# Attention beside a long convolution on one core: the opening in smaller pieces, with new numbers for the planner

## The chip, the core and the metric

The kernel runs on one core of a Trainium2 chip. The core has engines that each work through a list of instructions in order and meet at semaphores: TensorE (PE, matrix products into the eight PSUM banks), ScalarE (ACT, functions of single elements), VectorE (DVE, arithmetic on tiles), GpSimd (POOL, here for setting memory and starting transfers) and SyncE (SP, here for starting transfers). The metric is the time of one execution on the device in microseconds (us), as the median of several runs. The profile is of one further execution.

## The reference

Two independent blocks, each on 2,048 tokens with 512 features, whose results stand side by side in the output. The first is attention with 32 heads of 16 features; the second multiplies shifted keys by values and convolves the product along the tokens with one filter of length 2,048 for each feature.

```
qkv = (x @ wqkv) -> q, k, v        # 32 heads of 16 features
scores = q @ k^T * 16 ** -0.5      # 32 x 2048 x 2048
a = (softmax(scores) @ v) -> (2048, 512) @ wo

k_shift = sum over 4 taps of shifted k * shift_k
kv = k_shift * v
y = causal convolution of kv with ssm_k  (by FFT in the reference)
b = q * (y + kv * ssm_D)
out = concatenate(a, b)
```

The costly part is the exponential of the 32 x 2048 x 2048 scores.

## The kernel before, in words

**Tiling.** The scores are cut into 2,048 blocks of 128 keys by 512 queries of one head. Heads are processed in groups of four that sit 32 partitions apart, of which a key matmul uses one strip of 32; a pass `n` is one group of four heads with one block of 512 queries, and there are 32 passes. For each block PE computes scores (L775), an engine takes the exponential, and PE multiplies it with the values (L912), summing in bank `PVB` over the 16 key tiles. A column of ones beside the values gives the softmax's denominator in the same matmul; at the end of a pass DVE transposes the sums (L981), divides and transposes back.

**Two engines for the exponential.** ACT reads two or three banks at once (L800, tile `PT`), three banks for even steps and three for odd ones. DVE computes other blocks by an approximation in four operations (L861, L868 twice, L873, tile `PTD`); such a block's scores come either in bank `BGB`, beside the three of ACT, or in the place of ACT's third bank, so that ACT has two in that step.

**Work between.** Projections of later heads (L485, L494, L517), the shifted keys (L506), the convolution (L1127, as matmuls with filter rows that SP loads into `WR`) and the output projection (L1055) are placed on PE between score groups. Where room is left, filler matmuls of zeros (L1322) keep PE busy.

**What sets the order.** All instruction lists are written out when the kernel is built. A planner keeps a clock for each engine and goes through steps `T`: it emits a step's scores and its exponential (`emit_qk`), value products of the step two before (`pv_step`), perhaps one more block for DVE (`late_block`), background work (`emit_bg`), transfers (`release`) and filler (`warm_up`). Constants at the top of the file are its limits. `LATE_D` says how long PE may be held by a late block, `LATE` how long a DVE block must be done before its value product is placed, `OVER_C`, `HURRY`, `HALF`, `TURN` and `NEAR` by how much a piece of background work may run over, `OPEN` and `CLOSE` how early it is taken up, `GAP` and `T_DVE` where DVE blocks are allowed, `S_U` how much of other DVE work goes ahead of an urgent operation, `N_TAIL` how many last steps have two blocks alone, and `MOST_OP` how many pieces of the output projection a step of the end may take. In such a step of two blocks the third bank belongs to the output projection.

**The opening.** DVE sets `JNK` (for an early load of ACT's table) and a zero tile in `PT`; PE multiplies the zero tile eight times (`warm`, L624) and then spreads a pattern for the mask `MASK` (L632). ACT's queue loads the first 128 columns of the q and k weights, SP's queue transposes x's first 512 tokens into `xT` in two transfers of 256, then loads the v weights and the rest of x. `first` (L639) makes q of tokens 0 to 255 in bank 6, k of the same in bank 7, and q of tokens 256 to 511 in bank 5. DVE multiplies q by the mask for even and odd heads (L649), ACT copies the keys (L653). The first step's scores need keys and queries of tokens 0 to 255; the second step's also need queries 256 to 511 for even heads. Keys from 256 on come as a unit of background work (L494, copied at L542).

The transfers of x are issued by these lines:

```
    load_x(0, 2)
    h_wv = [dma(sp, d_w[2], WV[:, :, 0:128], wview[:, :, 2 * D:2 * D + 128], kb=128, late=1.8)]
    load_x(1)
    load_x(2)
    load_x(3)
```

## Time and profile before

| | us |
|---|---|
| median of 3 runs (lowest, highest) | 818.57 (818.21, 819.93) |
| the profiled execution | 822.45 |
| its span, first to last instruction | 820.71 |
| first exponential on ACT begins | 9.23 |
| last stretch of exponentials ends | 815.79 |
| exponentials on ACT, three blocks / two blocks | 456 / 202 |
| blocks on DVE | 276 |
| filler matmuls on PE | 602 |

The page shows busy time by engine, the chain of work that ended last, and the costliest groups of instructions. "Idle before" is the time in which an engine stood still ahead of an instruction, with the work that ended the wait. ACT is the fullest engine, so the time is read best as its list: when it begins, what its instructions take, where it stands still, and what follows the last one. PE waits for ACT before 447 groups of scores, 186.0 us in all: there the delay is PE's, and it costs nothing.

### The profile page before, as it was taken

How to read it: one execution, taken by the hardware profiler on the slowest of the kernel's cores; microseconds unless marked ns; L12 is line 12 of the kernel's file. 1: busy time of each engine (PE TensorE's matmuls, PEld its weight loads, DVE VectorE, ACT ScalarE, POOL GpSimd, SP SyncE). 2: the span in 40 equal slices, each digit the busy share in tenths (PEclk: the TensorE clock that was granted, in tenths of full speed). 3: DMA queues.
4: the chain of work that ended last, by engine and by line, in shares of the span. 5: the costliest groups of instructions: out<-in, count | busy, mean ns of one | idle time of the engine just before them, and what ended most of it. 6: DMA issues, size and time to landing. Idle time of an engine off the chain costs nothing.

```text
span 820.7 us, 31039 instructions
## 1 busy us (share of the span) xinstructions
PE 737.6 (90%) x14084; PEld 328.8 (40%) x14084; DVE 786.7 (96%) x1383; ACT 801.7 (98%) x662; POOL 87.6 (11%) x160
## 2 busy tenths in 40 slices
PE   8889999999987988989898999999989989999887
PEld 3333434444342443434443444344433333434244
DVE  4999999999997999999999999999999979999996
ACT  6999999999998999999999999999999999999997
POOL 6200211010100101000011010101001102010000
PEclk9999999999999999999999999999999999999999
DMA  9896077768577684265678286677787582663100
GB/s 233 187 299 194 8 162 253 263 194 270 190 267 257 236 280 150 53 205 186 237 236 266 72 266 239 229 258 244 259 254 240 181 279 93 214 221 109 53 2 28
DMA packets 88882, 161.39 MB, mean 197 GB/s; under 512 B 50256, under 2 KB 53968, under 8 KB 88368
## 3 DMA queue, kind: packets, MB, share of 16 engines
q1 hardware_dynamic: 81760, 150.43, 57.2%
q0 software_dynamic: 5792, 8.66, 3.5%
q8 instruction: 111, 1.82, 0.9%
q10 hardware_dynamic: 1200, 0.33, 0.2%
q14 instruction: 19, 0.16, 0.1%
HBM read 142.61 MB, written 6.42 MB: 182 GB/s over the span
## 4 chain that ended last, share of the span: by engine, by line
ACT 86%; DVE 6%; PE 5%; issue 1%; DMA 1%
ACT PT L800 86%; DVE EH L868 2%; PE PS L775 2%; DVE PTD L873 1%; DVE FX L861 1%; PE PS L912 1%; PE PS L1127 1%; DMA xT<-in_A_x_dram 1%; PE PS L494 0%; PE PS L639 0%; DVE OUTA L1063 0%; PE PS L517 0%; DVE DT L981 0%; PE PS L1055 0%; DVE YB L1147 0%
## 5 line engine op out<-in xcount | busy, mean ns | idle before, releaser
L800 ACT ACTIVATE PT<-PS 128x1536 bf16<-128x1536 f32 (+1 forms) x658 | 799.4, 1527 | 8.2 <-PE PS L775 7.9
L775 PE MATMUL PS<-QT,KTo 32*128 32x512 bf16 (+2 forms) x2248 | 261.4, 366 | 55.7 <-ACT PT L800 23.9
L912 PE MATMUL PS<-PT,VA 128*32 128x512 bf16 (+2 forms) x1948 | 195.6, 370 | 11.4 <-issue 6.1
L873 DVE SCALAR_TENSOR_TENSOR PTD<-EH,FX 128x512 uint16<-128x512 f32 x276 | 185.3, 677 | 5.2 <-PE PS L912 5.0
L861 DVE TENSOR_SCALAR FX<-PS 128x512 f32<-128x512 f32 x276 | 187.5, 681 | 2.0 <-PE PS L775 1.7
L868 DVE SCALAR_TENSOR_TENSOR EH<-EH 128x512 f32<-128x512 f32 x276 | 183.8, 677 | 0.0
L868 DVE SCALAR_TENSOR_TENSOR EH<-FX 128x512 f32<-128x512 uint16 x276 | 181.9, 682 | 0.1
L1127 PE MATMUL PS<-WR,KV 128*24 128x128 bf16 (+8 forms) x8192 | 171.5, 220 | 0.2 <-issue 0.2
L775 PEld LDWEIGHTS PS<-QT,KTo 32*128 32x128 bf16 x2248 | 68.5, 91 | 228.8 <-ACT PT L800 186.0
L1127 PEld LDWEIGHTS PS<-WR,KV 128*32 128x32 bf16 (+7 forms) x8192 | 135.5, 95 | 43.9 <-issue 21.7
L1322 PE MATMUL PS<-IDN,ZW 128*32 128x512 bf16 (+3 forms) x602 | 131.1, 313 | 1.5 <-DVE DT L981 1.2
L347 POOL DMA_DIRECT2D QT<-QS x120 | 58.4, 494 | 461.0 <-DVE QS L533 411.1
L912 PEld LDWEIGHTS PS<-PT,VA 128*32 128x32 bf16 x1948 | 49.3, 93 | 113.3 <-issue 94.8
L912 PE MATMUL PS<-PTD,VA 128*32 128x512 bf16 (+1 forms) x300 | 87.0, 369 | 1.7 <-DVE PTD L873 1.7
L1322 PEld LDWEIGHTS PS<-IDN,ZW 128*32 128x32 bf16 x602 | 49.2, 96 | 45.5 <-issue 14.9
L347 POOL DMA_DIRECT2D out_dram<-OUTA x15 | 8.2, 549 | 150.5 <-DVE OUTA L1063 144.2
L912 PEld LDWEIGHTS PS<-PTD,VA 128*32 128x32 bf16 x300 | 22.5, 95 | 3.5 <-DVE PTD L873 2.6
L981 DVE STREAM_TRANSPOSE DT<-PS 128x512 f32<-128x512 f32 x31 | 21.9, 707 | 1.5 <-PE PS L912 1.3
L517 PE MATMUL PS<-WKV,xT 128*128 128x128 bf16 x256 | 17.6, 220 | 2.2 <-DVE FX L861 0.9
L1147 DVE CAST YB<-PS 128x256 bf16<-128x256 f32 x32 | 13.4, 417 | 6.0 <-PE PS L1127 5.0
L494 PE MATMUL PS<-xT,WKV 128*128 128x512 bf16 (+1 forms) x64 | 17.6, 385 | 1.4 <-DVE KV L555 0.7
L1055 PE MATMUL PS<-WKV,OTN 128*128 128x512 bf16 (+1 forms) x68 | 18.0, 370 | 0.4 <-DVE OTN L1030 0.3
(69 smaller groups left out, 226.6 us busy)
## 6 DMA issues: line engine op xcount, KB each, us to landing
WR<-kz_scratch SPq DMA_DIRECT2D x256, 512.0 KB, 5.7
KV<-KV SPq DMA_DIRECT2D x16, 256.0 KB, 5.7
kz_scratch<-WR SPq DMA_DIRECT2D x1, 2176.0 KB, 8.3
QN<-in_B_q_dram POOLq DMA_DIRECT2D x2, 1024.0 KB, 8.6
out_dram<-QN POOLq DMA_DIRECT2D x2, 1024.0 KB, 8.5
QT<-QS POOLq DMA_DIRECT2D x120, 16.0 KB, 1.9
out_dram<-OUTA POOLq DMA_DIRECT2D x15, 128.0 KB, 2.2
QN<-in_B_ssm_k_dram SPq DMA_DIRECT2D x1, 1024.0 KB, 9.1
```

The costliest lines, as they stand in the source:

```text
L347: f(outp, inp).then_inc(dsem.sem, 16)
L494: return e.matmul(PS[:, bank, c0:512], lhsT=WK[:, dc, o * 128:(o + 1) * 128], rhs=xT[:, dc, sc * 512 + c0:(sc + 1) * 512], start=(dc == 0) ...
L775: ins = e.matmul(PS[:, bank, i * w:i * w + w], lhsT=KTo[32 * s:32 * s + 32, OF[n_] % 2, kt * 128:(kt + 1) * 128], rhs=QT[32 * s:32 * s + 3 ...
L800: h_exp[T] = act.op(lambda e: e.activation(PT[:, p0:p0 + n, :].rearrange("p b f -> p (b f)"), PS[:, banks[0]:banks[0] + n, :].rearrange("p ...
L861: h_f = urgent(lambda e: e.tensor_scalar(fx, PS[:, bank, :], FIX_ADD, FIX_HI, ALU.add, ALU.min), [h, h_last.get(i - R_FX)], slack=S_FX)
L868: st["h"] = dve.op(lambda e: e.scalar_tensor_tensor(eh, src, (P1, P2)[j], src, ALU.add, ALU.mult), [st["h"], h_last.get(i - R_EH)], us=us)
L873: lambda e: e.scalar_tensor_tensor(out16, eh, P3, fx, ALU.mult, ALU.add),
L912: ins = e.matmul(dst, lhsT=w, rhs=rhs, start=first, stop=last, tile_position=(0, 32 * s))
L981: h_t = urgent(lambda e: e.transpose(out=dt, in_=PS[:, PVB, :]), [h, h_mul.get(n - 1)], slack=S_T, us=(0.63, 0.751))
L1055: ins = e.matmul(PS[:, b, c0:c1], lhsT=OTN[:, PAIRS.index((o, qb)), t * 128:(t + 1) * 128], rhs=WO[:, o, c0:c1], start=(o == 0), stop=(o = ...
L1127: ins = e.matmul(PS[32 * g:32 * g + 2 * ((30 - d) // 2 + 1), BGB, c0:c0 + w], lhsT=kv, rhs=WR[:, (4 * qd + g) % R_W, S - 64 * d - 128:S - ...
L1322: pe.op(lambda e, s=s, k=k, rhs=rhs, bank=bank, rows=rows, c0=c0, first=first: e.matmul(PS[32 * s:32 * s + rows, bank, c0:c0 + 128 * k], l ...
```

## The change

The zero tile for the warm-up is a quarter as wide (the matmul reads its 128 columns four times), and is set before `JNK`. There are nine warm-up matmuls, two ahead of the mask's and seven behind them. x's first 512 tokens come in three transfers, of 128, 128 and 256 tokens. q and k of the first 256 tokens are made in halves of 128, in the order q, k, q, k. q of tokens 256 to 511 is made behind the first step's scores, in `more_q`, with the mask products that belong to it and those for odd heads. Fourteen constants of the planner have new values, so the order of the whole kernel differs.

```diff
-LATE_D = 0.4
+LATE_D = 1
-OVER_C = 0.0
-HURRY = 2
+OVER_C = 0.2
+HURRY = 4
-N_TAIL = 9
-MOST_OP = 2
+N_WARM = 9
+N_TAIL = 10
+MOST_OP = 3
-T_DVE = 5
+T_DVE = 6
-OPEN = 40
-CLOSE = 2
-S_U = 0.6
+OPEN = 30
+CLOSE = 12
+S_U = 0.5
-GAP = 5
+GAP = 6
-HALF = 0.25
-TURN = 0.2
+HALF = 0.35
+TURN = 0.05
-NEAR = 0.2
+NEAR = 0.1
-LATE = 0.3
+LATE = 0.1
...
-    load_x(0, 2)
+    load_x(0, (0, 128, 256, 512))
...
+    h_w0 = dve.op(lambda e: e.memset(PT[:, 0, 0:128], 0.0), us=(0.1, 0.2))
     h_j = dve.op(lambda e: e.memset(JNK[:], 0.0))
-    h_w0 = dve.op(lambda e: e.memset(PT[:, 0, 0:512], 0.0), us=(0.3, 0.4))
...
-    def warm(e):
+    def warm(e, n):
         ins = None
-        for _ in range(8):
-            ins = e.matmul(PS[:, 0, :], lhsT=PT[:, 0, 0:128], rhs=PT[:, 0, 0:512], start=True, stop=True)
+        for _ in range(n):
+            ins = e.matmul(PS[:, 0, :].rearrange("p (r n) -> p r n", r=4), lhsT=PT[:, 0, 0:128],
+                           rhs=PT[:, 0:1, 0:128].broadcast_to([128, 4, 128]), start=True, stop=True)
         return ins
-    pe.op(warm, [h_w0], run=2.6, kind="F")
+    pe.op(lambda e: warm(e, 2), [h_w0], run=0.64, kind="F")
...
+    pe.op(lambda e: warm(e, N_WARM - 2), [], run=0.32 * (N_WARM - 2), kind="F")
...
-    h_qa = first(PS[:, 6, 0:256], WQ, 0, 256, [h_x[0][0], h_wq[0]], 0.11)
-    hk = first(PS[:, 7, 0:KEYS0], WK, 0, KEYS0, [h_x[0][0], h_wk[0]], 0.11 * KEYS0 / 256)
-    h_qb = first(PS[:, 5, 0:256], WQ, 256, 512, [h_x[0][1], h_wq[0]], 0.11)
...
+    for i in range(2):
+        h_qa = first(PS[:, 6, 128 * i:128 * i + 128], WQ, 128 * i, 128 * i + 128, [h_x[0][i], h_wq[0]], 0.055)
+        hk = first(PS[:, 7, 128 * i:128 * i + 128], WK, 128 * i, 128 * i + 128, [h_x[0][i], h_wk[0]], 0.055)
+    turn_q(0, 0, 6, h_qa)
     h_k0 = bank_free[7] = act.op(lambda e: e.activation(KTo[:, 0, 0:KEYS0], PS[:, 7, 0:KEYS0], ACT.Copy), [hk], us=(0.28, 0.42))
+
+    def more_q():
+        h_qb = first(PS[:, 5, 0:256], WQ, 256, 512, [h_x[0][2], h_wq[0]], 0.11)
+        turn_q(0, 256, 5, h_qb)
+        turn_q(1, 0, 6, h_qa)
+        turn_q(1, 256, 5, h_qb)
...
         if T < end[0]:
             emit_qk(T)
+        if T == 0:
+            more_q()
         advance(pe.t)
```

`turn_q(par, c0, bank, hp)` is the mask product of one half for even (`par` 0) or odd heads, the same DVE operation as before (L649).

More of the change, by code (lines that the diff above doesn't have):

```diff
@@ L381, in bass_concat_heads__mha_block__ssm_conv_h3__prompt_kernel @@
     d_w = [DmaSem(sem(f"d_w{i}")) for i in range(6)]
-    d_x = [DmaSem(sem(f"d_x{i}")) for i in range(5)]
+    d_x = [DmaSem(sem(f"d_x{i}")) for i in range(6)]
     d_kv = [DmaSem(sem(f"d_kv{i}")) for i in range(7)]
@@ L395, in bass_concat_heads__mha_block__ssm_conv_h3__prompt_kernel, with load_x @@
     h_x = {}
-    def load_x(sc, parts=1):
-        w = 512 // parts
-        h_x[sc] = [dma(sp, d_x[sc + 4 * (i > 0)], xT[:, :, t0:t0 + w], x2[t0:t0 + w, :], transpose=True, kb=w, rate=X_KB, late=1.8)
-                   for i, t0 in enumerate(range(sc * 512, (sc + 1) * 512, w))]
+    def load_x(sc, cuts=(0, 512)):
+        h_x[sc] = [dma(sp, d_x[sc if i == 0 else 3 + i], xT[:, :, sc * 512 + c0:sc * 512 + c1], x2[sc * 512 + c0:sc * 512 + c1, :],
+                       transpose=True, kb=c1 - c0, rate=X_KB, late=1.8)
+                   for i, (c0, c1) in enumerate(zip(cuts, cuts[1:]))]
     h_wq = [dma(act, d_w[0], WQ[:, :, 0:128], wview[:, :, 0:128], kb=128, late=1.8)]
     h_wk = [dma(act, d_w[1], WK[:, :, 0:128], wview[:, :, D:D + 128], kb=128, late=1.8)]
-    load_x(0, 2)
+    load_x(0, (0, 128, 256, 512))
     h_wv = [dma(sp, d_w[2], WV[:, :, 0:128], wview[:, :, 2 * D:2 * D + 128], kb=128, late=1.8)]
@@ L641, in first, with turn_q @@
         return h
-    h_qa = first(PS[:, 6, 0:256], WQ, 0, 256, [h_x[0][0], h_wq[0]], 0.11)
-    hk = first(PS[:, 7, 0:KEYS0], WK, 0, KEYS0, [h_x[0][0], h_wk[0]], 0.11 * KEYS0 / 256)
-    h_qb = first(PS[:, 5, 0:256], WQ, 256, 512, [h_x[0][1], h_wq[0]], 0.11)
-    h_q[0], h_q[1] = [], []
-    for par in range(2):
-        for bank, c0, hp in ((6, 0, h_qa), (5, 256, h_qb)):
-            hh = bank_free[bank] = dve.op(
-                lambda e, par=par, bank=bank, c0=c0: e.tensor_scalar(QT[:, 0, par, c0:c0 + 256], PS[:, bank, 0:256], MASK[:, par:par + 1], None, ALU.mult),
-                [hp, h_mask], us=(0.335, 0.46))
-            h_q[(par, c0 // 256)] = hh
-        h_q[par] = hh
-    h_k0 = bank_free[7] = act.op(lambda e: e.activation(KTo[:, 0, 0:KEYS0], PS[:, 7, 0:KEYS0], ACT.Copy), [hk], us=(0.28, 0.42))
+    def turn_q(par, c0, bank, hp):
+        hh = bank_free[bank] = dve.op(
+            lambda e: e.tensor_scalar(QT[:, 0, par, c0:c0 + 256], PS[:, bank, 0:256], MASK[:, par:par + 1], None, ALU.mult),
+            [hp, h_mask], us=(0.335, 0.46))
+        h_q[(par, c0 // 256)] = hh
+        if c0:
+            h_q[par] = hh
+    for i in range(2):
+        h_qa = first(PS[:, 6, 128 * i:128 * i + 128], WQ, 128 * i, 128 * i + 128, [h_x[0][i], h_wq[0]], 0.055)
+        hk = first(PS[:, 7, 128 * i:128 * i + 128], WK, 128 * i, 128 * i + 128, [h_x[0][i], h_wk[0]], 0.055)
+    turn_q(0, 0, 6, h_qa)
+    h_k0 = bank_free[7] = act.op(lambda e: e.activation(KTo[:, 0, 0:KEYS0], PS[:, 7, 0:KEYS0], ACT.Copy), [hk], us=(0.28, 0.42))
+    def more_q():
[3 more added lines that the diff above has]
+        turn_q(1, 256, 5, h_qb)
     NBLK = NQB * NG * KT * 4
```

## Prediction

> **What bounds the kernel now.** I read the page first: its busy times and its chain by engine.

> ```profile
> PE 737.6 (90%) x14084; PEld 328.8 (40%) x14084; DVE 786.7 (96%) x1383; ACT 801.7 (98%) x662; POOL 87.6 (11%) x160
> ...
> ACT 86%; DVE 6%; PE 5%; issue 1%; DMA 1%
> ```

> ScalarE (ACT) works for 801.7 of 820.7 us, and the chain runs over it for 86% of the span. VectorE (DVE) is nearly as full, so work cannot simply be handed to it. Next I asked for ACT's instructions alone, in order of time; each row is a stretch without a gap (start, length, count, and in brackets the idle time before it).

> ```profile
> 9.23 10.43 ACT L800 ACTIVATE PT<-PS 128x1536 bf16<-128x1536 f32 x8 [1.02 <-PE PS L775]
> 20.11 236.91 ACT L800 ACTIVATE PT<-PS 128x1536 bf16<-128x1536 f32 x194 [0.45 <-PE PS L775]
> 260.56 2.37 ACT L800 ACTIVATE PT<-PS 128x1536 bf16<-128x1536 f32 x2 [3.54 <-PE PS L775]
> 263.46 20.43 ACT L800 ACTIVATE PT<-PS 128x1536 bf16<-128x1536 f32 x17 [0.53 <-PE PS L775]
> ...
> 668.34 136.37 ACT L800 ACTIVATE PT<-PS 128x1536 bf16<-128x1536 f32 x110 [0.20 <-PE PS L775]
> 805.02 10.77 ACT L800 ACTIVATE PT<-PS 128x1536 bf16<-128x1536 f32 x11 [0.31 <-PE PS L775]
> ```

> So the span is four things: 9.23 us until the first exponential, the exponentials back to back, nine gaps (0.45, 3.54, 0.53, 0.44, 0.67, 0.19, 0.52, 0.20, 0.31: 6.85 us), and 820.71 - 815.79 = 4.9 us behind the last one. The price of one exponential comes from the groups by shape in two of the stretches:

> ```profile
> L800 ACT ACTIVATE PT<-PS 128x1536 bf16<-128x1536 f32 x138 | 203.5, 1679 | 0.5 <-PE PS L775 0.5
> L800 ACT ACTIVATE PT<-PS 128x1024 bf16<-128x1024 f32 x56 | 70.2, 1275 | 0.0
> ...
> L800 ACT ACTIVATE PT<-PS 128x1536 bf16<-128x1536 f32 x83 | 118.9, 1729 | 0.2 <-PE PS L775 0.2
> L800 ACT ACTIVATE PT<-PS 128x1024 bf16<-128x1024 f32 x27 | 31.9, 1182 | 0.0
> ```

> 138a + 56b = 236.91 and 83a + 27b = 136.37 give a = 1.345 us for three blocks and b = 0.916 for two: 0.429 a block and 0.058 an instruction. Each gap costs about 0.12 more than its length, the drain of the instruction before it. Last, the opening in order of time, and the chain at the long gap:

> ```profile
> 1.29 3.59 PE L624 MATMUL PS<-PT 128*128 128x512 bf16 x8 [1.29 <-DVE PT L427]
> 5.91 1.03 PE L639 MATMUL PS<-xT,WQ 128*128 128x256 bf16 x4 [0.88 <-DMA xT<-in_A_x_dram]
> 6.73 1.06 PE L639 MATMUL PS<-xT,WKV 128*128 128x256 bf16 x4
> 7.59 1.06 PE L639 MATMUL PS<-xT,WQ 128*128 128x256 bf16 x4
> 7.83 0.38 ACT L653 ACTIVATE KTo<-PS 128x256 bf16<-128x256 f32 x1 [4.50 <-PE PS L639]
> 8.58 0.61 PE L775 MATMUL PS<-QT,KTo 32*128 32x256 bf16 x6
> 10.08 0.39 PE L775 MATMUL PS<-QT,KTo 32*128 32x256 bf16 x6
> ```

> ```profile
> 255.53 3.56 issue
> ```

> The key copy ends at 8.21, but the scores start at 8.58: until 8.44 PE still does q of tokens 256 to 511 (four matmuls from 7.59, 0.213 apart). That 0.213 for 256 columns is half rate; from 10.08 the same shape takes 0.11. The long gap is PE's sequencer standing still for 3.56 us with nothing to wait for.

> **The change, opening first.** (1) The zero tile is set before JNK and with a quarter of the columns: PE's first matmul moves from 1.29 to about 1.04 (0.88, when DVE begins, plus some 0.10 for the set, as JNK's 0.06 and the old 0.27 suggest, plus the 0.06 seen from 1.23 to 1.29). Nine warm-up matmuls at 0.427 apiece and the mask's two (some 0.25) last until 5.13. (2) Of x's first 256 tokens, each half now feeds four q and four k matmuls of 128 columns. The old transfer landed at 5.86, the one issued behind it at 6.67, both weights by 5.58. I take 5.86 for the second half: the same bytes through the same queue; it could come up to 0.81 later, the distance of those two landings. (3) q of tokens 256 to 511 goes behind the first scores.

> At half rate: q and k of the first half 5.13 to 6.0 (k's weights land at 5.58, in time), of the second until 6.86 (eight times 0.107). The key copy starts 0.24 later, as before (7.59 to 7.83), at 7.10 and ends at 7.48; scores at 7.6 instead of 8.58; first exponential at 8.25 instead of 9.23. But the second chunk's scores need the moved q: 8.16 to 9.01 on PE, 0.24 to DVE, 0.43 there, scores at 9.8, exponential at about 10.4 against 10.58 before. So at half rate the gain shrinks to some 0.15: the stall has moved to the second exponential. At full rate from 5.1 on: k done at 6.35 (x at 5.90 plus 0.45), copy 6.55 to 6.93, scores 7.05, moved q 7.4 to 7.84, DVE until 8.5, scores 8.6, exponential 9.05: gain 1.53. Which holds? Before, full rate came by 10.08, about 4.1 us into matmuls that ran almost without a break from 5.91; the eight warm-ups were 3.4 us and had 1.2 us of near idleness behind them. Now matmuls run unbroken from 1.04 for 5.8 us, so I put the rate nearer to full: 0.15 + 0.8 x 1.38 = 1.25 us gained, ends +0.66 (half rate and x 0.81 late: a loss) and -1.6.

> [...]

> (4) SP issues one transfer more. Issues took 1.36 and 1.28 us for 256 tokens, 2.60, 2.28 and 2.67 for 512, so the fixed part of one is 0 to 0.4. Behind it stand the v weights and x of the other 1,536 tokens; x's next 512 landed at 9.55 and were used at 11.73, so 0.4 is covered even with everything 1.25 earlier; without that cover each late piece would hold PE, and then ACT, for the rest. [...]

> **The planner's numbers.** In the instruction lists of the two built kernels ACT has 481 exponentials of three blocks and 165 of two, instead of 456 and 202; DVE has 275 blocks instead of 276. ACT: (481 - 456) x 1.345 - 37 x 0.916 = -0.27, say -0.3 us. DVE loses four operations of 0.6 us: nothing, since ACT bounds. PE has 149 fewer filler matmuls (55,040 fewer columns, 23 us at 0.216 for 512): nothing either, as long as PE keeps ahead of ACT, for which it waits 447 times before scores, 186 us in all (0.42 each). One thing is new: 15 chunks get a block's scores for DVE as a matmul group by itself, of which before shows none in the steady part. The work behind the last exponential (output projection's last piece, DVE's four short operations, copy and store) stands as it was: 0, bounds +/-0.3. For the gaps of the steady part I take no change: causes (sequencer stalls, a late block, a bank not free) remain, at new places; bounds -3.5 to +4.8, worked out below.

> **The sum.** The profiled execution took 822.45 (span 820.71 and 1.74 around it), 3.88 over the median 818.57: just about its long gap. Without it and its sequel: 822.45 - (3.54 + 0.12) - (0.53 + 0.12) = 818.14, a little under the lowest timed run (818.21). Then -1.25 (opening) and -0.3 (ACT): **816.6**; its own range 815.6 to 817.6 from the opening's ends near it.

> **Rivals.** *Late blocks (slower):* at the 15 new places PE may stand for DVE's bank, up to the allowed 1 us instead of 0.4, and the next chunk's scores come late behind it, since PE works in order. A gap costs 0.53 (mean of the eight short ones, 3.31/8, plus drain). Six such gaps eat the gain and 0.2% more; nine make 816.6 + 4.8 = 821.4. For it: DVE is 96% busy. Against: the 0.42 of slack.
> *Fewer gaps:* seven short gaps of 2.78 us and 0.84 of drain remain in the sum; if two thirds go, 814.2. For it: new bounds of the planner exactly where DVE and PE meet; against: most follow sequencer stalls.
> *Opening gives back its gain* (half rate): 816.6 + 1.1 = 817.7. For it: the eight warm-ups had no effect on the rate.
> *A long sequencer stall in the timed runs too:* 816.6 + 4.3 = 820.9. For it: one execution in four showed it, as far as times tell.
> [...]

> **From this to the numbers.** Chances: forecast 0.40, late blocks 0.16, fewer gaps 0.20, opening given back 0.14, long stall 0.07, split 0.03. A run tells no change from one of up to 0.2% (1.64 us: 816.9 to 820.2). Faster: two thirds of the forecast, all of "fewer gaps", a little of the third, 0.48. Slower: most of late blocks and of the stall, 0.20. Same: the rest, 0.32. Range 813.8 to 821.2: from just below "fewer gaps" to just short of the worst late blocks.

> **What would show it.** First exponential at 7.5 to 8.3 us, second without a gap over 0.9, k matmuls 0.107 or 0.056 apart; 646 exponentials of 1.345 and 0.916; gaps of ACT summing to 2 to 4 us, none behind a single-block score group; 4.9 us behind the last. I am wrong if the opening is at 9 us or later, or if ACT's gaps exceed 6 us without a long sequencer stall.

## The result, and the profile after

The changed kernel is slower: median 828.46 us (826.59 to 830.42, six runs) against 818.12 (817.70 to 819.93) for the kernel before in the same measurement; the ratio is 1.0123, with a 95% interval of 1.0103 to 1.0143. The forecast was 816.6, and its range ended at 821.2. The profiled execution took 830.42 us, its span 828.5.

First the page after: busy times, TensorE's granted clock in tenths for 40 slices of the span, and the chain by engine.

```profile
PE 746.6 (90%) x13944; PEld 331.6 (40%) x13944; DVE 785.7 (95%) x1379; ACT 803.4 (97%) x650; POOL 87.6 (11%) x160
...
PEclk9999999989989897999999999999999999999989
...
ACT 71%; DVE 18%; PE 9%; issue 1%
```

ACT's work is the same to 2 us, as forecast. What is new is in the clock's row: five slices under 9, where before had none. This is the row before:

```profile
PEclk9999999999999999999999999999999999999999
```

The mean granted clock is 0.967 instead of 0.996, and in all six runs it lay between 0.967 and 0.977. The chain leaves ACT for 29% of the span instead of 14%.

ACT's list in order of time after; each row is a stretch, the bracket the idle time before it.

```profile
7.95 1.45 ACT L810 ACTIVATE PT<-PS 128x1536 bf16<-128x1536 f32 x1 [0.50 <-PE PS L785]
10.25 1.45 ACT L810 ACTIVATE PT<-PS 128x1536 bf16<-128x1536 f32 x1 [0.85 <-PE PS L785]
12.01 1.45 ACT L810 ACTIVATE PT<-PS 128x1536 bf16<-128x1536 f32 x1 [0.31 <-PE PS L785]
14.17 25.20 ACT L810 ACTIVATE PT<-PS 128x1536 bf16<-128x1536 f32 x19 [0.70 <-PE PS L785]
39.98 145.53 ACT L810 ACTIVATE PT<-PS 128x1536 bf16<-128x1536 f32 x117 [0.61 <-PE PS L785]
186.12 1.45 ACT L810 ACTIVATE PT<-PS 128x1536 bf16<-128x1536 f32 x1 [0.61 <-PE PS L785]
188.11 51.40 ACT L810 ACTIVATE PT<-PS 128x1536 bf16<-128x1536 f32 x42 [0.54 <-PE PS L785]
...
318.03 4.26 ACT L810 ACTIVATE PT<-PS 128x1536 bf16<-128x1536 f32 x3 [1.33 <-PE PS L785]
...
585.25 33.81 ACT L810 ACTIVATE PT<-PS 128x1536 bf16<-128x1536 f32 x27 [1.90 <-PE PS L785]
...
625.33 165.11 ACT L810 ACTIVATE PT<-PS 128x1536 bf16<-128x1536 f32 x134 [1.19 <-PE PS L785]
```

The first exponential starts at 7.95 instead of 9.23 (-1.28 us), but three gaps of 1.86 us follow at once, where before had one of 0.45. Behind the opening there are 19 gaps of 12.1 us in all, against eight of 6.4. ACT's stretches add up to 801.7 us instead of 799.7. So the ledger is -1.28 (start) + 7.1 (gaps) + 2.0 (stretches) = 7.8 us, the difference of the spans. Of the 2.0, the changed counts of exponentials should give -0.3 and the drain of 13 gaps more (0.12 each) 1.6; the other 0.7 us is not explained.

Where do the gaps stand? The clock was at half rate in eight stretches of the steady part, 51 us together (before: two, 6.8 us), and 11.0 of the 12.1 us of gaps lie in such a stretch or just behind one. Here is one of them in windows as long as a step of the clock. Each row has the window's length, the busy time and number of instructions of PE, its weight loads, DVE, ACT and POOL, then the granted clock and the DMA traffic.

```profile
174.20:177.60 3.40, 3.40 (x125) 1.96 (x113) 3.40 (x7) 3.40 (x4) 0.00 (x0) 1.00 0.82 233
177.60:181.00 3.40, 2.73 (x39) 0.90 (x23) 3.40 (x7) 3.40 (x4) 0.00 (x0) 1.00 0.92 320
181.00:184.40 3.40, 3.30 (x17) 0.63 (x16) 3.40 (x6) 3.40 (x4) 0.00 (x0) 0.51 1.02 343
184.40:187.90 3.50, 3.50 (x30) 1.87 (x26) 2.22 (x5) 2.56 (x2) 0.00 (x0) 0.50 0.91 346
```

PE issues 39 matmuls in the second window, the clock is halved for the next two, and in the last of them ACT works 2.56 of 3.50 us. (PE's busy column counts modelled ends; PE streams columns in only half of the second window, 0.51 by the count of the last section.) This is what PE and DVE do in the second window:

```profile
178.50 0.09 PEld L785 LDWEIGHTS PS<-QT,KTo 32*128 32x128 bf16 x1 [0.23 <-DVE YB L1157]
...
178.93 0.69 DVE L871 TENSOR_SCALAR FX<-PS 128x512 f32<-128x512 f32 x1
...
179.68 0.40 PE L1169 MATMUL PS<-IDN,YB 128*128 128x128 bf16 x4 [0.52 <-DVE FX L871]
```

At 178.5 a late block's scores have waited until DVE copied the convolution's result (YB) out of bank 7. The late block takes the bank at once, and the convolution's transpose (L1169), next in PE's list, must wait until DVE's first operation (FX) has read it: bank 7 is waited for twice within 1.5 us.

### The profile page after: what moved, and what is told of

Its sections match the earlier page's. It is cut to its first block, busy times and chain, and to the rows that moved or that the text cites. A ratio compares the mean times of both kernels' runs of the same rounds, so it can differ in the third digit from the quotient of the medians.

```text
span 828.5 us, 30667 instructions
## 1 busy us (share of the span) xinstructions
PE 746.6 (90%) x13944; PEld 331.6 (40%) x13944; DVE 785.7 (95%) x1379; ACT 803.4 (97%) x650; POOL 87.6 (11%) x160
## 4 chain that ended last, share of the span: by engine, by line
ACT 71%; DVE 18%; PE 9%; issue 1%
ACT PT L810 71%; DVE EH L878 8%; DVE FX L871 4%; DVE PTD L883 4%; PE PS L785 3%; PE PS L922 2%; PE PS L1332 1%; PE PS L486 1%; PE PS L1137 1%; PE PS L625 0%; DVE DT L991 0%; PE PS L495 0%; DVE YB L1157 0%; DVE KTo L543 0%; DVE QN L1176 0%
## 5 line engine op out<-in xcount | busy, mean ns | idle before, releaser
L785 PE MATMUL PS<-QT,KTo 32*128 32x512 bf16 (+2 forms) x2248 | 288.4, 373 | 56.4 <-ACT PT L810 21.0
L922 PE MATMUL PS<-PT,VA 128*32 128x512 bf16 (+2 forms) x1949 | 199.9, 378 | 9.1 <-DVE DT L991 3.7
L1137 PE MATMUL PS<-WR,KV 128*22 128x128 bf16 (+9 forms) x8192 | 171.3, 220 | 1.9 <-issue 1.8
L785 PEld LDWEIGHTS PS<-QT,KTo 32*128 32x128 bf16 x2248 | 74.1, 91 | 238.8 <-ACT PT L810 151.7
L1137 PEld LDWEIGHTS PS<-WR,KV 128*20 128x20 bf16 (+7 forms) x8192 | 136.8, 95 | 40.9 <-issue 20.6
L1332 PE MATMUL PS<-IDN,ZW 128*32 128x512 bf16 (+3 forms) x453 | 103.8, 321 | 0.1
L1332 PEld LDWEIGHTS PS<-IDN,ZW 128*32 128x32 bf16 x453 | 37.2, 98 | 40.0 <-issue 22.7
L486 PE MATMUL PS<-xT,WQ 128*128 128x512 bf16 x60 | 18.8, 445 | 1.2 <-DVE FX L871 1.2
L518 PE MATMUL PS<-WKV,xT 128*128 128x128 bf16 x256 | 19.5, 226 | 0.3
```

The costliest lines, as they stand in the source:

```text
L486: return e.matmul(PS[:, bank, :], lhsT=WQ[:, dc, o * 128:(o + 1) * 128], rhs=xT[:, dc, qb * 512:(qb + 1) * 512], start=(dc == 0), stop=(dc ...
L518: ins = e.matmul(PS[:, bank, 128 * j:128 * j + 128], lhsT=xT[:, dc, (4 * sc + j) * 128:(4 * sc + j + 1) * 128], rhs=WV[:, dc, o * 128:(o + ...
L785: ins = e.matmul(PS[:, bank, i * w:i * w + w], lhsT=KTo[32 * s:32 * s + 32, OF[n_] % 2, kt * 128:(kt + 1) * 128], rhs=QT[32 * s:32 * s + 3 ...
L922: ins = e.matmul(dst, lhsT=w, rhs=rhs, start=first, stop=last, tile_position=(0, 32 * s))
L1137: ins = e.matmul(PS[32 * g:32 * g + 2 * ((30 - d) // 2 + 1), BGB, c0:c0 + w], lhsT=kv, rhs=WR[:, (4 * qd + g) % R_W, S - 64 * d - 128:S - ...
L1332: pe.op(lambda e, s=s, k=k, rhs=rhs, bank=bank, rows=rows, c0=c0, first=first: e.matmul(PS[32 * s:32 * s + rows, bank, c0:c0 + 128 * k], l ...
```

## The experiments

Each was timed in rounds against the kernel before on the same chip. The kernel before itself had medians of 819 to 820 us there, its runs from 815 to 825, so ratios are given, with 95% intervals.

**Taking the change apart.**

```diff
 # e1: the changed kernel
-LATE_D = 1
+LATE_D = 0.4
 # e4: the kernel before
-LATE_D = 0.4
+LATE_D = 1
-S_U = 0.6
+S_U = 0.5
```

e2 is the kernel before with all the new numbers; e3 is the changed kernel with the old ones, but S_U 0.5.

> The changed kernel with one number put back: LATE_D 0.4, with which no block's scores are placed late (a late block needs at least 0.216 + 2 x 0.105 = 0.426 us). Theory A (late blocks: PE stands for bank 7, its activity in a window of some 3.4 us falls under about half, the clock goes to half rate, and exponentials stand): 90 late blocks gone, about 817 to 819 us, at most three cold windows in the steady part, granted clock 0.99 or more. Rival B (the other twelve planner numbers make the low windows): still 825 to 830, clock about 0.97. Rival C (the opening's new order shifts the whole and is to blame): also 825 to 830.

> The kernel before with the fourteen new planner numbers and the old opening. Theory A: 94 late blocks, so still slow, 825 to 831 us, clock about 0.97, six or more cold windows. Rival C (opening): back to 817 to 820. Rival B: slow as well; so this run tells A and B from C.

> The new opening with the planner's old numbers, but S_U 0.5 as in the changed kernel (with 0.6 the plan breaks an assertion of its own). No late blocks. Theory A: 816.5 to 819; the opening itself gains at most 0.3 us at the second exponential, since its scores wait for bank 5, which the two mask products of the moved q hold. Rival C: 824 or more. Rival B: about 817 to 819 like A.

> The kernel before with LATE_D 1 (and S_U 0.5, without which the plan breaks its own assertion): 77 late blocks, all else old. Theory A: slow, 823 to 829 us, five or more cold windows, clock 0.97 to 0.98. Rivals B and C: 817 to 820.

| | ratio (95%) | granted clock, all runs | half rate in the profile |
|---|---|---|---|
| before | 1 | 0.987 to 1.000 | 6.8 us |
| changed | 1.0123 (1.0103 to 1.0143) | 0.967 to 0.977 | 54.6 |
| e1, late blocks off | 1.0024 (0.9996 to 1.0052) | 0.992 to 1.000 | 10.2 |
| e2, old opening | 1.0046 (1.0011 to 1.0081) | 0.967 to 0.992 | 20.5 |
| e3, opening alone | 1.0102 (1.0049 to 1.0155) | 0.991 to 0.998 | 6.8 |
| e4, late blocks alone | 1.0066 (1.0043 to 1.0088) | 0.975 to 0.985 | 41.0 |

The clock obeys theory A: it is low with late blocks and not without. The time does not quite. e2 has 94 late blocks and took 822.8 us, where 825 to 831 was expected; it has no twin without late blocks, so what they cost in its plan stays open. And e3 has no late block and a good clock, and is slow all the same: 829.0 us, where 816.5 to 819 was expected. Its waits of PE for its own sequencer are 14.1 us (pauses of 0.25 us and more), in 16 places, against 1.8 in the changed kernel and 6.1 in the kernel before. So time is lost in a second way, and it can come with a new plan. That had to be measured by itself.

These stalls can be set beside the transfers. The page lists a queue that brings instructions, in packets of 16 KB (packets, MB, share):

```profile
q8 instruction: 109, 1.79, 0.8%
```

Behind the first 20 us the 20 profiles hold 78 sequencer stalls of 0.7 us or more, and every one of them ends 1.2 to 1.6 us after such a packet has landed; of moments drawn at random, 6% do. That PE waits in these stalls for the next part of its instruction list is my estimate from these landings; no run shows it by itself. How many stalls there are, and how long, differs from plan to plan (14.1, 1.8 and 6.1 us above).

**How good was the plan before?** Four kernels are the kernel before with one planner number changed: T_DVE 6 (e9), GAP 6 (e10), LATE 0.1 (e11), OPEN 30 (e12). None has a late block, and the engines' work is the same to a few instructions.

> The kernel before with T_DVE 6 alone: another plan of the same kind (657 steps, no late block, 276 blocks on DVE, 662 filler matmuls). Theory P (the plan before was an unusually good one, and any other plan with the same engines' work loses to sequencer stalls and short waits at new places): 821 to 827, clock 0.99 or more. Theory A alone (only late blocks cost): 817 to 820 and clock 0.99 or more.

> The kernel before with GAP 6 alone: another plan again (658 steps, no late block, 278 blocks on DVE). Theory P: 821 to 827. Theory A alone: 817 to 820. In both the clock at 0.99 or more.

> The kernel before with LATE 0.1 alone (a DVE block's value product may be planned 0.1 us after its exponential instead of 0.3): 656 steps, no late block. Theory P: 821 to 827, with more PE waits for the last DVE operation of a block. Theory A alone: 817 to 820. Clock 0.99 or more in both.

> The kernel before with OPEN 30 alone (background work taken up at most 30 steps early instead of 40): 655 steps, no late block. Theory P: 821 to 827. Theory A alone: 817 to 820. Clock 0.99 or more in both.

Ratios: 1.0169 (1.0102 to 1.0237), 1.0006 (0.9982 to 1.0030), 1.0041 (1.0017 to 1.0066), 1.0033 (1.0000 to 1.0065); clock 0.986 to 1.000. The worst, e9, by PE's waits and by ACT's list:

```profile
PE PS L1127 <- issue: 14.9, 9, 4.1
...
573.13 1.02 ACT L800 ACTIVATE PT<-PS 128x1024 bf16<-128x1024 f32 x1 [4.31 <-PE PS L775]
575.24 1.45 ACT L800 ACTIVATE PT<-PS 128x1536 bf16<-128x1536 f32 x1 [1.08 <-PE PS L775]
```

In its profiled execution, the slowest of its four, PE stood nine times before the convolution's matmuls, up to 4.1 us, with nothing to wait for but its sequencer, and the mean granted clock was 0.986: the gap of 4.31 is the stall, and the 1.08 behind it I put down to the clock. Theory P expected 821 to 827 us: e11 (823.7) and e12 (824.8) lie there, though e12's interval reaches down to no loss; e9 (833.2) is worse, and e10 (819.7) loses nothing. So a new plan can lose up to 1.7% without a late block, and none of the four is faster than the plan before. A single comparison of two plans therefore proves little, and the late blocks needed pairs.

**Late blocks in pairs.** Two more pairs are the changed kernel with one other number (GAP 5; OPEN 40), with and without `LATE_D = 0.4`.

> The changed kernel with GAP 5: another plan with 80 late blocks. If late blocks cost time on average: clock 0.965 to 0.985 and at least 3 us more than its twin with LATE_D 0.4 on the same chip; 822 to 830. If plans alone decide: no such order between the twins.

> The twin: GAP 5 and LATE_D 0.4, no late block. If late blocks cost time: clock 0.99 or more, 817 to 823, at least 3 us less than the twin with them.

> The changed kernel with OPEN 40: 87 late blocks. If late blocks cost time on average: clock 0.965 to 0.985, at least 3 us over its twin without them; 823 to 831. If plans alone decide: no such order.

> The twin: OPEN 40 and LATE_D 0.4, no late block. If late blocks cost time: clock 0.99 or more, 817 to 824, at least 3 us under the twin with them.

| pair | with late blocks | clock | without | clock |
|---|---|---|---|---|
| changed, e1 | 1.0123 | 0.967 to 0.977 | 1.0024 | 0.992 to 1.000 |
| e14, e15 | 1.0114 (1.0058 to 1.0171) | 0.969 to 0.988 | 1.0030 (1.0003 to 1.0057) | 0.993 to 0.998 |
| e16, e17 | 1.0095 (1.0064 to 1.0126) | 0.967 to 0.989 | 1.0016 (0.9986 to 1.0045) | 0.985 to 0.998 |

Three times the same order: late blocks cost 0.8 to 1.0 points, some 7 us, and without them these plans are within 0.3% of the kernel before.

Does this cost go with the clock? The executions of one kernel differ in both. A straight line through the changed kernel's six runs gives 4.2 us more for each 0.01 of clock less (correlation -0.97), and, extended to the full clock, an estimate of 816.8 us; the 115 runs of the kernel before beside the experiments give 6.5 us (-0.83) and 817.0. So nearly all that the changed kernel loses goes along with its clock. That alone does not say which causes which, since a standstill of PE can go with both at once, as in e9 (a stall of 4.1 us, a gap of 4.31 on ACT, a clock of 0.986).

**What of a late block costs?** e5 allows none while the transpose of the convolution is due. e6 adds filler where the plan has PE wait for bank 7. e13 keeps the changed kernel's plan and only moves 69 fillers in front of such waits (the semaphore counts that the other engines wait for are renumbered to match). e18 has LATE_D 0.6, which allows a late block only where bank 7 is almost free.

```diff
 # e5
-        if T not in chunks or T >= end[0] or len(queue) <= LAST_BLKS or len(chunks[T]) > 3:
+        if state["turn"] or T not in chunks or T >= end[0] or len(queue) <= LAST_BLKS or len(chunks[T]) > 3:
 # e6
+        fill_wait(BGB)
         h = qk_mm([(extra, BGB)])
...
+        fill_wait(bank)
         h = pe.op(fn, [bank_free[bank], h_ybw[0], h_idn], run=0.223, kind="F")
 # e13, behind the plan
+                place_of[j] = i - 0.9 + 0.001 * (j - i)
 # e18
-LATE_D = 1
+LATE_D = 0.6
```

> The changed kernel, but no late block in a step where a transpose of the convolution's result waits for bank 7. 68 late blocks stay. In five of the nine low windows of the changed kernel that transpose stood behind a late block's first DVE operation (0.2 to 0.8 us in each; 10 such waits, 6.0 us in all). Theory A1 (the pile-up of two waits for bank 7 makes the low windows): these waits fall under 2 us, cold time in the steady part from 51 us to under 25, 820 to 824 us. Theory A2 (late blocks as such, through 19 us of scores in which three of PE's four row strips do nothing and which take the place of filler): cold time stays over 35 us, 825 to 829.

> The changed kernel with filler matmuls of zeros put in front of a late block's scores and of that transpose where the plan has PE wait for bank 7 by 0.2 us or more (35 of them); 77 late blocks stay. If the low clock comes from PE standing idle at bank 7, cold time falls under 25 us and the time to 820 to 824, though late blocks and their waits stay. If the waits themselves cost the time and the clock only goes along with them, the time stays at 825 to 829 even where the clock is better.

> The changed kernel's own plan, instruction for instruction, except that 69 of its 453 filler matmuls stand some places earlier, in front of a late block's scores or of the convolution's transpose, where the plan has PE wait for bank 7; nothing is added, all other engines' lists are the same. If the low clock is the cost: granted clock from 0.97 to 0.985 or more, cold time in the steady part from 51 to under 30 us, time 819 to 824. If the plan's other accidents cost the time: 826 to 830 whatever the clock.

> The changed kernel with LATE_D 0.6: 56 late blocks, only where bank 7 is free within some 0.17 us, so that the plan has them wait 0.6 us in all instead of 10.8. If the waits cost: clock 0.99 or more, 818 to 823. If the lone scores themselves cost (0.216 us each on PE, and less filler): clock under 0.985, 824 or more.

| | late blocks | ratio (95%) | clock, mean of runs |
|---|---|---|---|
| changed | 90 | 1.0123 (1.0103 to 1.0143) | 0.972 |
| e5, none at the transpose | 68 | 1.0039 (1.0001 to 1.0076) | 0.987 |
| e6, filler added | 77 | 1.0083 (1.0051 to 1.0114) | 0.989 |
| e13, filler moved | 90 | 1.0112 (1.0039 to 1.0184) | 0.974 |
| e18, no planned wait | 56 | 1.0037 (1.0010 to 1.0064) | 0.994 |

e18 settles the main question: 56 late blocks whose planned waits are 0.6 us in all, instead of 10.8, leave the clock at 0.994 and the time near e1's. Their smaller number does not explain it: in proportion to 90, 56 blocks would have cost 0.6 points over e1, and 0.13 were measured, with some 0.3 of uncertainty on each ratio. PE's waits of the transpose for DVE's FX (sum, times, longest), in the changed kernel and in e18:

```profile
PE PS L1169 <- DVE FX L871: 6.0, 10, 1.2
```

```profile
PE PS L1169 <- DVE FX L871: 2.1, 4, 0.8
```

e5, which forbids just that meeting, has most of the gain as well. But filling the wait was no cure. e13 moved filler there from places nearby; these waits fell only to 3.2 us, and the clock stayed (0.974). e6 added some; the waits fell to 1.5 us and the clock rose to 0.989, but the time stayed at 825.8 us. Ahead of the run that outcome was to mean that the waits themselves cost the time and the clock only goes along. Its profile does not decide it: 9.9 of the 11.8 us of ACT's gaps behind the opening still lie in stretches of half rate or just behind one, and the longest, 3.20 us, comes where a value product waits 2.74 us for a DVE block. So what helped was a plan without the wait; how much of the cost comes by way of the clock, and how much directly, stays open.

**Filler and the clock.** e8 is the kernel before with less filler.

```diff
-BUSY = 0.85
+BUSY = 0.6
```

> The kernel before with BUSY 0.6 instead of 0.85: 224 filler matmuls instead of 602, no late blocks, nothing else meant. If it is PE's activity in a window of 3.4 us that holds the clock, many more windows lie under half: clock under 0.96, over 60 us of half rate, 828 us or more. If filler does nothing for the clock: 817 to 820 and clock 0.99.

Clock 0.973 to 0.987, half rate for 34 us, ratio 1.0034 (1.0007 to 1.0061): with 224 fillers instead of 602 the clock was lower than before (0.987 to 1.000, 6.8 us), but the expected 828 us and the clock under 0.96 did not come. Why 34 us of half rate cost so little here is not shown. It may be that PE has time to spare in this plan; but between e8's own runs 0.01 of clock goes with 3.9 us (correlation -0.63), about as in the changed kernel, so its plan may also be better in other ways.

**The moved q.** e7 is e1 with the moved q in the free half of bank 6, where its mask products then read it.

```diff
-        h_qb = first(PS[:, 5, 0:256], WQ, 256, 512, [h_x[0][2], h_wq[0]], 0.11)
+        h_qb = first(PS[:, 6, 256:512], WQ, 256, 512, [h_x[0][2], h_wq[0]], 0.11)
...
```

> The changed kernel with LATE_D 0.4 and the moved q in the free half of bank 6 instead of bank 5. If the second step's scores waited for bank 5 (held until the last mask product), the second exponential comes at 9.1 to 9.5 us instead of 10.1 to 10.3, and the gap ahead of it shrinks from 0.95 to under 0.3; if they waited for the mask product that they read, it stays over 10. The total: 816 to 820, if no other place is hit.

The opening of the changed kernel, then of e7, in order of time:

```profile
7.84 0.61 PE L642 MATMUL PS<-xT,WQ 128*128 128x256 bf16 x4
...
8.49 1.27 DVE L647 TENSOR_SCALAR QT<-PS,MASK 128x256 bf16<-128x256 f32 x3 [1.35 <-PE PS L642]
...
9.81 0.39 PE L785 MATMUL PS<-QT,KTo 32*128 32x256 bf16 x6 [1.15 <-DVE QT L647]
```

```profile
8.34 1.27 DVE L647 TENSOR_SCALAR QT<-PS,MASK 128x256 bf16<-128x256 f32 x3 [1.20 <-PE PS L642]
...
8.88 0.40 PE L785 MATMUL PS<-QT,KTo 32*128 32x256 bf16 x6 [0.36 <-DVE QT L647]
```

In the changed kernel the second step's scores start behind all three mask products (8.49 + 1.27 = 9.76), though they read only the first: the second step writes banks 3, 4 and 5, and bank 5 holds the moved q until the last product has read it. With bank 6 they start behind the first product, and the second exponential at 9.32 instead of 10.25. The total (824.6 us, where 816 to 820 was expected; ratio 1.0077, 1.0046 to 1.0109) is worse than e1's: again another plan, with ACT's gaps elsewhere. PE's waits for its sequencer are 5.3 us instead of 4.6, which does not explain the difference.

## Why the prediction was wrong

**The planner's numbers, the step that failed.** "nothing either, as long as PE keeps ahead of ACT" priced 149 fewer fillers and the late blocks at nothing. Two things were missed. The number: I counted 15 score groups standing by themselves in the instruction list, but a late block whose scores directly follow its step's own looks like a group of four there; counted while the list is made there are 90 (before: none, since by the planner's numbers a late block needs 0.216 + 2 x 0.105 = 0.426 us and LATE_D was 0.4). And the kind of cost: the slack of 0.42 us a step was taken as the only guard, while PE's standing still came here with a lower clock as well (0.967 to 0.977 in the changed kernel, 0.992 to 1.000 in e1), so that a delay of PE ahead of ACT could not be taken as free. PE's scores after took 288.4 us instead of 261.4. The three pairs put the late blocks at some 7 us, and e5 and e18 put it down to their waits for bank 7.

**The rival on the slow side** had the place and the sign (PE stands for DVE's bank at late blocks, scores come late), at 0.16 and 821.4. Its price per gap (0.53, drain included) was below the 0.64 + 0.12 seen on average (12.1/19 and the drain). The number of gaps was wrong too: it took nine at 15 places, while 16 of the 19 stand in or just behind eight stretches of half rate, two to a stretch.

**The gaps of the steady part** were taken as unchanged; that a plan is another draw, from 0 to 1.7% worse (e9 to e12), was not in the range at all. Bounds of -3.5 to +4.8 from the gaps of one good plan were too narrow for that. The rivals of fewer gaps and of a long stall are out: 22 gaps instead of nine, and PE's longest sequencer stall is 1.4 us.

**The opening.** First exponential at 7.95: in the forecast's 7.5 to 8.3. x's first 256 tokens in two transfers: k's matmuls ran from 5.55 on without a wait for x. The 0.03 for the split stood for a fixed cost of one transfer more, and no run shows one by itself: the two transfers landed at 4.76 and 5.07, 0.31 us apart, against 5.86 for the one of 256 tokens before. Nine warm-ups: q and k of the first 256 tokens still ran at half rate (0.107 apart), and full rate came at 7.0, before any score but not at the 5.1 of the better case. The steps of the clock in this trace stand multiples of 3.41 us apart. In the eleven profiles with this opening (all but e7's) full rate came at 3.95 to 7.34 us, a spread of 3.4, and the first exponential at 7.21 to 8.11. With the old opening, in eight profiles, they came at 4.25 to 10.04 and at 7.51 to 9.32. So the profile before was a late draw, and part of the 1.28 us between the two profiles is luck; the means, 8.53 and 7.68, differ by 0.85.

But the sum needed 1.25 us at the second exponential, and that came at 10.25, where 9.05 was forecast at full rate. The step left out is that bank 5 is held by the moved q. Behind the wait of 1.15 us for it the clock was halved from 10.4 to 13.8, and by the fourth exponential (14.17 against 13.24) the opening was behind the kernel before. Not every run with that wait has the fall: e3, with its windows 0.8 us earlier, kept full rate and had its fourth exponential at 12.70; e7, without the wait, at 12.01. On average the fourth exponential stands at 13.25 in the eleven and at 12.53 in the eight. As far as single executions of plans that differ in more than the opening tell, the new opening thus loses some 0.7 us instead of gaining 1.25. The rival in which the opening gives back its gain had the outcome, at another place than it named.

**ACT's own work and the end** were right: 481 and 165 exponentials, and 4.9 us behind the last.

## What to carry to other kernels

When a planner's numbers change, treat the whole order as new: first ask what one number switches on (here a limit of 0.4 that nothing could meet became 1), and count what it emits in the planner and not in the list. Waits of TensorE that ACT's queue was to hide went here with a lower clock (0.967 to 0.989 with late blocks, 0.985 to 1.000 without, over the three pairs) and some 7 us, so price a bank by everything that stands in line for it. Compare such changes in pairs over several plans, since plans with the same work differ here by up to 1.7%, and an opening over several executions, since full rate came anywhere from 3.95 to 10.04 us in these profiles.

## What the runs showed of the hardware

```
share of the window   windows   next one at half rate
under 0.35                 23        22
0.35 to 0.40               25        14
0.40 to 0.45               65        15
0.45 to 0.50              118         8
0.50 to 0.55              259         4
0.55 and more            3338         0
```

The mean share is 0.66. Of the 23 windows with a share under 0.35, 22 were followed by half rate, and of the 3,338 with 0.55 and more none; 41 of the 63 windows ahead of half rate had a share of 0.35 to 0.55. What brought full rate back cannot be read from these runs: counted at half the pace, the windows that ended a fall had shares of 0.59 to 0.92, and those behind which it went on 0.43 to 0.87. A fall lasted one to three windows, 3.4 to 10.2 us, in these profiles.
